# Attention and two mixtures of experts on one core: turns of the last batch behind P·V, the second mixture's first weights split during attention, first labels made in the tail

## The chip, the core and the metric

The program runs on one core of a Trainium2 chip. The metric is the device time in microseconds (us) of one execution, the median of several runs.

## The reference

Attention over 4 batches, 8 heads, 576 positions of 64 features, with a window of 32 (heads 0 to 3) or of 32 positions at a distance of 4 (heads 4 to 7); then a mixture in which every token goes to one expert by a greedy choice with a capacity; then a second mixture in which every token goes through all experts with balanced weights.

```python
scores = where(mask, q @ k.T / 8, -1e9)           # 4 x 8 x 576 x 576
x = softmax(scores) @ v                           # to 2304 tokens x 512
logits = x @ w_gate                               # 8 experts, 288 tokens each
for idx in argsort(-logits.flatten()):            # highest logit first
    ... token takes the expert if both are free
x = relu(x @ w1[e]) @ w2[e]                       # first mixture, e: the token's
P = exp(x @ w_gate2); 8 rounds of row and column normalization
out = sum over e of P[:, e] * (relu(x @ w1b[e]) @ w2b[e])   # second mixture
```

## The kernel before

All instructions are written out in order by hand (`manual_schedule`): each engine works through its own queue in program order, and waits come from the data that an instruction needs or the buffer that it writes. DMAs of SyncE (SP), ScalarE and GpSimd stand in the queue of the engine that issues them.

*Attention* works on 25 units. Unit u holds 96 queries of one block for the plain heads (kind 0, block u − 1) and 96 for the dilated heads (kind 1, block u), so that units 18 to 24 hold the last batch. The loop over n is a software pipeline: in step n come `scores(n)` (masks and q·k on TensorE), `row_max(n)` (the maximum and its product with −0.125, `nm`, on VectorE), `p_trans(n - 1)` and `p_evac(n - 1)` (transposes of the exponentials and their copy to `pt`), `exps(n)` (eight exponentials on ScalarE), `pv(n - 2)` (P·V, 16 matmuls, and the normalized rows `xt` on VectorE), and `x_out(n - 3)`, which splits `xt` into two f16 halves `xo`, the high one copied on ScalarE, the low one subtracted on GpSimd, and stores them to `xd` in DRAM. `xo` has two buffers. PSUM is divided among scores (`ps_s`, two), transposes (`ps_p`, one) and P·V (`ps_v`, one).

The q and k of all four batches are loaded ahead of the loop, `v` of two batches, the rest of `v` in steps 8, 9, 14, 15. Tokens' rows come back transposed from `xd` by a DMA transpose (`x_load`) for the first three batches, and `logits` of 128 tokens (12 matmuls) follow P·V in the steps after. For the last batch `x_turn` transposes `xo` on TensorE and copies it to `xl` on ScalarE. It does so for two units at a time at the end (`TURN`: in steps 24, 25 and 27; unit 22 in step 26). The last five chunks of logits are copied to `L` together.

*Routing.* `Router.phase(ph)` finds the tokens of one expert: labels (lines 455 to 460: the best logit `m` of each token, its expert as a code, the mask `A` of tokens), then six passes of a search for a threshold: G (line 476) compares `m` with 64 or 32 thresholds in two halves on VectorE, 18 matmuls count (line 480), `ok` compares the counts, a matmul hands `ok` to all partitions (line 485), `pen` and `cur` choose (lines 488 to 490). After the passes come the expert's index `widx` and the tokens' index `idx`.

*The mixtures* (`Moe.stage1`). During phase 0 TensorE has warming matmuls (`warm`, zeros) between the yields, and `weights` splits the first six of eight pieces of the second mixture's first expert: a DMA of 512 KB into `raw` (four buffers), the high half on ScalarE (line 679), the low one on VectorE (line 680). Then come gathers of the first mixture's weights (line 700) and of `x` (line 709) on GpSimd, 16 warming matmuls, and the first mixture's layers (`moe1`, line 731 the matmuls), interleaved with the next routing phase and the splits of the weights, the last two pieces of the second mixture's among them.

Of the kernel before, what the change touches and what calls it, by code (L numbers as in the profile page):

```python
# [83 lines left out]
TURN = {NU - 1: (NU - 7, NU - 6), NU: (NU - 5, NU - 4), NU + 2: (NU - 2, NU - 1)}  # L84
# [22 lines left out]
def attention(tc, q, k, v, masks, wg, ident, xd, L, zero):  # L107

    nc = tc.nc
    with ExitStack() as ctx:  # L110
# [24 lines left out]
        negc = one.tile([QB, 2, 4], F32)  # L135
        nc.gpsimd.memset(negc, -SC)
# [40 lines left out]
        def row_max(u):  # L177
            p, gs = SS[u], part(u, 4)
            nm = wk.tile([QB, 2, 4], F32, name="nm")
            nc.vector.tensor_reduce(nm[:, :, gs], p[:, :, gs], axis=AX.X, op=OP.max)  # L180
            nc.vector.tensor_mul(nm[:, :, gs], nm[:, :, gs], negc[:, :, gs])
            PP[u] = nm

        def exps(u):
            p, nm, gs = SS.pop(u), PP[u], part(u, 4)
            e = wk.tile([QB, 2, 4, 128], F32, name="e")
            for s in range(2):
                for g in range(gs.start, gs.stop):
                    nc.scalar.activation(e[:, s, g, :], p[:, s, g, :], AF.Exp, bias=nm[:, s, g:g + 1], scale=SC)
            PP[u] = e  # L190
# [15 lines left out]
        def pv(u, extra):  # L206
# [9 lines left out]
            fin = [logits(p[:, 0, 480 + E * n:480 + E * (n + 1)], c) for n, c in enumerate(extra)]  # L216
            rc = wk.tile([QB, 2, 4, 1], F32, name="rc")
            xt = wk.tile([QB, 2, 4, D], F32, name="xt")
# [4 lines left out]
            for f in fin:  # L223
                f()

        def x_out(u):
            xt, ks = XT.pop(u), part(u, 2)
            if u in XO:
                xo = XO[u]
            else:  # L230
                xo = wk.tile([QB, 2, 2, 4, D], F16, name="xo")
# [10 lines left out]
        def x_turn(*units):  # L242

            for u in units:
                p = ps.tile([128, 2, 512], F32, name="ps_s").bitcast(F16)[:, :, :4 * QB].rearrange(
                    "p k (c q) -> p k c q", c=4)
                ks = part(u, 2) if u > (B - 1) * NJ else slice(1, 2)
                for kind in range(ks.start, ks.stop):
                    for c in range(4):
                        nc.tensor.transpose(p[:, kind, c, :], XO[u][:, kind, c // 2, 2 * (c % 2):2 * (c % 2) + 2, :],  # L250
                                            idh)
                for kind in range(ks.start, ks.stop):
                    for o, n, tok, st in tokens_of(QB * UNITS[u][kind][1], QB, kind):
                        nc.scalar.activation(xl[kind][:, :, tok:tok + st * (n - 1) + 1:st], p[:, kind, :, o:o + n],
                                             AF.Copy)

        XB, XO = {}, {}
# [8 lines left out]
        def left(c, a, x):  # L266

            t0 = 128 * c - S * (B - 1)
            if x == 0:
                return XB[c][:, a, :]  # L270
            return xl[a // 4][:, a % 4, max(t0, 0):t0 + 128]

        def logits(p, c):
            cut = S * (B - 1) - 128 * c
            for x, rows in ((0, slice(0, min(cut, 128))), (1, slice(max(cut, 0), 128))):
                n = 0
                for kt in range(4 if rows.start < rows.stop else 0):
                    hi = kt if kt < 2 else kt + 2
                    for a, w in ((hi, wgh), (hi, wgl), (hi + 2, wgh)):
                        nc.tensor.matmul(p[rows], left(c, a, x), w[:, kt, :], start=(n == 0), stop=(n == 11))  # L280
# [7 lines left out]
        for b in range(1, B if True else 2):  # L288
            for kind in (1, 0):
                for nm in "kq":  # L290
                    load_qk(nm, b, kind)
            if b == 1:
                for kind in (1, 0):
                    load_v(b, kind)
        nc.scalar.activation(wgh, wgf, AF.Copy, scale=SG)
        nc.vector.scalar_tensor_tensor(wgl, wgf, SG, wgh, op0=OP.mult, op1=OP.subtract)
        xl = [one.tile([128, 4, S], F16, name="xl%d" % kind) for kind in range(2)]
        for n in range(NJ + 1):
            XO[(B - 1) * NJ + n] = one.tile([QB, 2, 2, 4, D], F16, name="xo%d" % n)
        first = S * (B - 1) // 128  # L300
        for n in range(NU + 3):
# [5 lines left out]
            if n < NU:  # L307
                exps(n)
            if n in FILL:
                warm(FILL[n])  # L310
            if n == NU + 1:
                x_turn(NU - 3)
            if 2 <= n <= NU + 1:
                pv(n - 2, [loaded.pop(0)[1] for _ in range(1 if n < NU else 2) if loaded and loaded[0][0] <= n])
# [3 lines left out]
            if n >= 3:  # L318
                x_out(n - 3)
# [9 lines left out]
            x_turn(*TURN.get(n, ()))  # L329
        p = ps.tile([128, 2, 512], F32, name="ps_v", bufs=1)  # L330
        rest = [i for _, i in loaded] + list(range(first, NT))
# [61 lines left out]
class Router:  # L393
# [39 lines left out]
    def start(self, ctx):  # L433
        self.wk = ctx.enter_context(self.tc.tile_pool(name="r_wk", bufs=2))

    def psum(self):
        return self.ps.tile([128, 512], F32, name=self.tag[0], bufs=self.tag[1])

    def phase(self, ph):
# [10 lines left out]
        if not last:  # L450
            m = wk.tile([128, NC], F32, name="m")
            w = wk.tile(full, F16, name="w")
            wm = wk.tile([128, NC], F32, name="wm")
            A = wk.tile(full, F16, name="A")
            V.tensor_reduce(m, Lm, axis=AX.X, op=OP.max)
            V.tensor_tensor(w, Lm, bc(m), op=OP.is_equal)
            V.tensor_mul(w, w, be(code))
            V.tensor_reduce(wm, w, axis=AX.X, op=OP.max)
            V.tensor_add(wm, wm, self.mask)
            V.tensor_tensor(A, w, bc(wm), op=OP.is_equal)  # L460
            cur, o = None, 0
            for n, bits in enumerate(STEPS):
# [8 lines left out]
                G = wk.tile([128, NC * 64], F16, name="G")[:, :NC * T].rearrange("p (c t) -> p c t", c=NC)  # L471
                p = self.psum()
                for h in range(2):
                    s = slice(h * NC // 2, (h + 1) * NC // 2)
                    sh = [128, NC // 2, T]
                    V.tensor_tensor(G[:, s], m[:, s].unsqueeze(2).to_broadcast(sh),
                                    c.unsqueeze(1).to_broadcast(sh), op=OP.is_ge)
# [126 lines left out]
class Moe:  # L604
    def __init__(self, ctx, tc, router, xd, ident, w1a, w2a, wg2, w1b, w2b, out, ps, zero):
        nc = self.nc = tc.nc
        self.tc, self.r, self.xd, self.out, self.ps = tc, router, xd, out, ps
# [3 lines left out]
        self.big, self.raw, self.sm = pool("m_big", 1), pool("m_raw", 4), pool("m_s", 1)  # L611
# [3 lines left out]
        self.acc = self.big.tile([128, NT, DM], F32, name="acc")  # L615
# [6 lines left out]
        self.W, self.balanced, self.scattered = {}, False, []  # L622
        self.wb = [[self.big.tile([128, 4, 7, 256], F16, name="w%d%s" % (n, c)) for c in "hl"] for n in (1, 2)]
# [11 lines left out]

    def psum(self):
# [692 lines left out]
```

## Time and profile before

| | us |
|---|---|
| median of 3 runs | 1833.92 (1832.78 to 1834.39) |
| profiled execution | 1835.58 |
| its span | 1833.8 |
| TensorE busy in it | 1752.4 (96%) |
| VectorE | 1371.8 (75%) |
| ScalarE | 838.0 (46%) |
| GpSimd | 226.7 (12%) |

The span runs from the first instruction to the last of the profiled execution; 1.78 us of its own time lie around it. The mean granted clock of TensorE is 0.979 of full speed. In the rows PE is TensorE's matmuls (PEld its weight loads), DVE VectorE, ACT ScalarE, POOL GpSimd, SP SyncE, and L174 line 174 of the kernel. Busy shares are means over stages with different limits. Attention fills about the first 127 us, the first routing phase ends near 162, and all that follows is the two mixtures.

### The profile page before, as it was taken

How to read it: one execution, taken by the hardware profiler on the slowest of the kernel's cores; microseconds unless marked ns; L12 is line 12 of the kernel's file. 1: busy time of each engine (PE TensorE's matmuls, PEld its weight loads, DVE VectorE, ACT ScalarE, POOL GpSimd, SP SyncE). 2: the span in 40 equal slices, each digit the busy share in tenths (PEclk: the TensorE clock that was granted, in tenths of full speed). 3: DMA queues.
4: the chain of work that ended last, by engine and by line, in shares of the span. 5: the costliest groups of instructions: out<-in, count | busy, mean ns of one | idle time of the engine just before them, and what ended most of it. 6: DMA issues, size and time to landing. Idle time of an engine off the chain costs nothing.

```text
span 1833.8 us, 35303 instructions
## 1 busy us (share of the span) xinstructions
PE 1752.4 (96%) x14518; PEld 1296.9 (71%) x14518; DVE 1371.8 (75%) x2625; ACT 838.0 (46%) x1502; POOL 226.7 (12%) x284
## 2 busy tenths in 40 slices
PE   8986898899999899999999999999999999999998
PEld 6873666676677657777777777777777777777776
DVE  5977776676744868887887888788878878887565
ACT  4662333333344345564544555444555544554333
POOL 1224222332221000000000000000000000000111
PEclk9987999999999999999999999999999999999999
DMA  8654322443343323434244432344352353433020
GB/s 304 149 137 134 114 83 77 127 119 94 87 142 94 88 82 150 152 132 160 99 167 178 170 139 108 154 155 157 131 205 101 109 213 147 155 132 151 35 96 35
DMA packets 106161, 241.19 MB, mean 132 GB/s; under 512 B 46704, under 2 KB 70512, under 8 KB 99088
## 3 DMA queue, kind: packets, MB, share of 16 engines
q1 hardware_dynamic: 84736, 151.34, 23.8%
q0 software_dynamic: 20592, 87.53, 13.7%
q8 instruction: 113, 1.85, 0.4%
q14 instruction: 48, 0.39, 0.1%
q10 hardware_dynamic: 672, 0.08, 0.0%
HBM read 173.83 MB, written 61.73 MB: 128 GB/s over the span
## 4 chain that ended last, share of the span: by engine, by line
PE 70%; issue 11%; DVE 10%; ACT 4%; DMA 3%; POOL 2%; SPq 0%; POOLq 0%; ACTq 0%; DVEq 0%
PE mm L995 26%; PE mm L1033 23%; PE mm L731 8%; PE mm L812 5%; PE mm L768 2%; PE ps_v L215 1%; DVE hl L952 1%; DVE w1l L680 1%; PE r L480 1%; PE ps_p L197 1%; PE ps_s L174 1%; POOL out_dram L1047 1%; ACT w1h L679 1%; DMA wgf<-in_wg_dram 1%; DMA rawk<-in_k_dram 1%
## 5 line engine op out<-in xcount | busy, mean ns | idle before, releaser
L995 PE MATMUL mm<-xb,w1h 128*128 128x384 f16 x2352 | 574.6, 327 | 5.9 <-DVE mm L966 5.0
L1033 PE MATMUL mm<-w2h,hh 128*128 128x256 f16 x1764 | 481.0, 273 | 1.3 <-DVE t L1057 1.2
L1033 PE MATMUL mm<-w2h,hl 128*128 128x256 f16 x1764 | 481.0, 273 | 0.0
L1033 PE MATMUL mm<-w2l,hh 128*128 128x256 f16 x1764 | 481.0, 273 | 0.0
L995 PE MATMUL mm<-xb,w1l 128*128 128x384 f16 x1176 | 384.2, 327 | 0.0
L1033 PEld LDWEIGHTS <-hh 128*128 128x128 f16 x3528 | 345.2, 98 | 43.9 <-issue 1.8
L995 PEld LDWEIGHTS <-w1h 128*128 128x128 f16 x2352 | 230.3, 98 | 160.9 <-issue 12.8
L1033 PEld LDWEIGHTS <-hl 128*128 128x128 f16 x1764 | 172.6, 98 | 20.0
L952 DVE TENSOR_TENSOR hl<-r,hh 128x1536 f16<-128x1536 f32 x84 | 147.5, 1756 | 42.4 <-ACT hh L951 42.4
L995 PEld LDWEIGHTS <-w1l 128*128 128x128 f16 x1176 | 115.2, 98 | 76.5 <-issue 0.7
L947 ACT ACTIVATE r<-mm 128x384 f32<-128x384 f32 x252 | 118.8, 480 | 96.8 <-PE mm L995 96.8
L951 ACT ACTIVATE hh<-r 128x1536 f16<-128x1536 f32 x84 | 124.6, 1483 | 48.4 <-DVE r L976 46.5
L913 POOL DMA_DIRECT2D ws<-raw x48 | 25.9, 541 | 945.4 <-ACT raw L864 724.2
L958 ACT ACTIVATE mm<-mm 128x384 f32<-128x384 f32 x84 | 40.3, 480 | 177.2 <-PE mm L995 177.2
L952 DVE TENSOR_TENSOR hl<-S,hh 128x1152 f16<-128x1152 f32 x84 | 113.5, 1352 | 0.0
L731 PE MATMUL mm<-xt,w1h 128*128 128x288 f16 x512 | 97.0, 289 | 1.4 <-ACT xt L745 1.4
L1043 DVE SCALAR_TENSOR_TENSOR acc<-t,P,acc 128x512 f32<-128x512 f32 x126 | 94.7, 752 | 4.5
L734 ACT ACTIVATE w1h<-mm 128x288 f16<-128x288 f32 (+1 forms) x120 | 46.8, 397 | 109.1 <-PE mm L731 91.0
L951 ACT ACTIVATE hh<-S 128x1152 f16<-128x1152 f32 x84 | 96.3, 1147 | 0.0
L735 DVE SCALAR_TENSOR_TENSOR w1l<-mm,w1h 128x288 f16<-128x288 f32 (+1 forms) x120 | 50.6, 436 | 56.2 <-ACT w1h L734 52.6
L864 ACT ACTIVATE raw<-raw 128x1024 f16<-128x1024 f32 x48 | 50.6, 1055 | 87.3 <-DVE raw L849 45.3
L731 PE MATMUL mm<-x2l,w0h 128*128 128x256 f16 x288 | 81.0, 281 | 8.4 <-DVE x2l L773 8.4
(258 smaller groups left out, 2970.0 us busy)
## 6 DMA issues: line engine op xcount, KB each, us to landing
xb<-xw SPq DMA_DIRECT2D x30, 1344.0 KB
ws<-raw POOLq DMA_DIRECT2D x48, 448.0 KB
ws<-r POOLq DMA_DIRECT2D x48, 448.0 KB
raw<-in_w2b_dram SPq DMA_DIRECT2D x32, 512.0 KB
raw<-in_w1b_dram SPq DMA_DIRECT2D x56, 256.0 KB
w1h<-ws SPq DMA_DIRECT2D x6, 1792.0 KB
w1l<-ws SPq DMA_DIRECT2D x6, 1792.0 KB
w2h<-ws SPq DMA_DIRECT2D x6, 1792.0 KB
```

Source lines behind the costliest of these rows:

```text
L731: nc.tensor.matmul(p, a[:, k, 128 * f:128 * (f + 1)], rhs(k, b), start=(k == 0 and i == 0), stop=(k == KT - 1 and i == 2))
L734: nc.scalar.activation(h[0][:, f, :n], p, AF.Relu)
L735: nc.vector.scalar_tensor_tensor(h[1][:, f, :n], p, 0.0, h[0][:, f, :n], op0=OP.max, op1=OP.subtract)
L812: nc.tensor.matmul(p, a[:, f, c], b[:, f, :], start=(f == 0 and n == 0), stop=(f == FT - 1 and n == 2))
L864: self.nc.scalar.activation(hi[:, k], x, AF.Copy, scale=sw)
L947: nc.scalar.activation(o, p, AF.Relu, scale=SH)
L951: yield nc.scalar.activation(hq[0][:, i, k], x, AF.Copy)
L952: yield V.tensor_sub(hq[1][:, i, k], x, hq[0][:, i, k])
L958: nc.scalar.activation(Q[i], P[i], AF.Copy)
L995: nc.tensor.matmul(p, w[u][:, 2 * j + i // 2, k, 128 * (i % 2):128 * (i % 2 + 1)], x[:, v, r, j], start=(q in (1, 5) and j == 0 and n == 0 ...
L1033: nc.tensor.matmul(p, h[u][:, i, a, 128 * t:128 * (t + 1)], w[v][:, i, b, :], start=(q in (1, 7) and i == 0 and j == 0), stop=(q in (2, 3) ...
L1043: V.scalar_tensor_tensor(self.acc[:, r, :], x, self.P[:, r, e:e + 1], self.acc[:, r, :], op0=OP.mult, op1=OP.add)
```

## The change

Before the loop of attention only the q and k of two batches are loaded, into two buffers each; the other two batches' are loaded in steps 6, 7, 12 and 13. `xo` has four buffers, `xt` three. `nm`'s product moves to ScalarE. `exps` yields after each half of its exponentials, and `x_out` stands between the halves. `x_turn` now transposes `xt` (f32) of one unit into free columns of a P·V or other PSUM bank and makes both f16 halves from there: copies on ScalarE, subtractions on VectorE. The turns of units 18 to 22 stand in `pv` of the unit after each (steps 21 to 25); those of 23 and 24 follow the loop. Chunks 13 and 14 of the logits may join the loop.

`first_weights` splits all eight pieces of the second mixture's first expert in attention: loads from step 4 on, then per step one half (512 columns) on ScalarE and the half before on VectorE. `Router.early` makes the labels and the first G of half of the columns between the last two turns; phase 0 makes the other half. `Moe` is made ahead of attention, with its load of `idf` and the copy `id16` on GpSimd. In phase 0 the splits go, and so do the single warming matmuls; three stand where five stood. Six stand where 16 stood ahead of the first mixture.

```diff
 def load_qk(nm, b, kind):
-    x = raw[nm, b, kind] = one.tile([128, 2, S], F32, name="raw%s%d%d" % (nm, kind, b))
+    x = raw[nm, b, kind] = ld.tile([128, 2, S], F32, name="raw%s%d" % (nm, kind))
...
 def row_max(u):
-    nc.vector.tensor_mul(nm[:, :, gs], nm[:, :, gs], negc[:, :, gs])
+    nc.scalar.activation(nm[:, :, gs], nm[:, :, gs], AF.Copy, scale=-SC)
...
-def pv(u, extra):
+def pv(u, extra, turn=None):
...
     fin = [logits(p[:, 0, 480 + E * n:480 + E * (n + 1)], c) for n, c in enumerate(extra)]
+    halves = x_turn(turn, p) if turn is not None else None
...
     for f in fin:
         f()
+    if halves is not None:
+        halves()
...
 def x_out(u):
+    xo = wk.tile([QB, 2, 2, 4, D], F16, name="xo", bufs=4)
     nc.scalar.activation(xo[:, ks, 0], xt[:, ks], AF.Copy)
-    eng = nc.gpsimd if u + 2 < NU else nc.vector
-    eng.tensor_sub(xo[:, ks, 1], xt[:, ks], xo[:, ks, 0])
+    nc.gpsimd.tensor_sub(xo[:, ks, 1], xt[:, ks], xo[:, ks, 0])
...
+def x_turn(u, p):
+    p = p[:, :, 264:264 + 2 * QB].rearrange("p k (c q) -> p k c q", c=2)
+    ks = part(u, 2) if u > (B - 1) * NJ else slice(1, 2)
+    for kind in range(ks.start, ks.stop):
+        for c in range(2):
+            nc.tensor.transpose(p[:, kind, c, :], XT[u][:, kind, 2 * c:2 * c + 2, :], idf[:QB, :QB])
...
+    def halves():
+        for n, (o, i, x) in enumerate(parts):
+            if x == 0:
+                nc.scalar.activation(o, i, AF.Copy)
+            else:
+                nc.vector.tensor_sub(o, i, hi[n - len(hi)])
+    return halves
...
-for b in range(1, B if True else 2):
-    for kind in (1, 0):
-        for nm in "kq":
-            load_qk(nm, b, kind)
+for kind in (1, 0):
+    for nm in "kq":
+        load_qk(nm, 1, kind)
...
-for n in range(NU + 3):
+for n in range(NU + 2):
...
-    if n < NU:
-        exps(n)
+    ex = exps(n) if n < NU else iter(())
+    next(ex, None)
+    turn = n - 3 if NU - 4 <= n <= NU else None
+    more = [loaded.pop(0)[1] for _ in range(1 if n < NU else 3) if loaded and loaded[0][0] <= n] if n >= 2 else []
+    if turn is not None:
+        pv(n - 2, more, turn)
+    if 3 <= n <= NU:
+        x_out(n - 3)
+    for _ in ex:
+        pass
     if n in FILL:
         warm(FILL[n])
...
+    if n >= 2 and turn is None:
+        pv(n - 2, more)
+    if 4 <= n:
+        next(side, None)
...
+    b, c = divmod(n - NJ, NJ)
+    if 0 <= b < B - 2 and c < 2:
+        for nm in "kq":
+            load_qk(nm, b + 2, 1 - c)
...
-    x_turn(*TURN.get(n, ()))
+    if n == NU:
+        loaded += [(n, i) for i in (first, first + 1)]
+turns = [x_turn(NU - 2, ps.tile([128, 2, 512], F32, name="ps_s")),
+         x_turn(NU - 1, ps.tile([128, 2, 512], F32, name="ps_p", bufs=1))]
+turns[0]()
+early()
+turns[1]()
+x_out(NU - 2)
+x_out(NU - 1)
...
 class Router:
+    def early(self):
+        half = slice(0, NC // 2)
+        self.pre = self.label_tiles(), self.grid(1 << STEPS[0])
+        self.labels(*self.pre[0], half)
+        self.above(self.pre[1], self.pre[0][0], self.thr[:, :1 << STEPS[0]].bitcast(F32), half)
...
 class Moe:
+    def first_weights(self, ctx):
...
+        for n in range(2):
+            load(n)
+        yield
+        for n in range(2, 4):
+            load(n)
+        yield
+        for n, (lay, k, per, m) in enumerate(todo):
+            r = live.pop(0).rearrange("p k f -> p (k f)")
+            hi, lo = (t[:, k:k + per, :].rearrange("p k f -> p (k f)") for t in self.W[("b", 0), lay])
+            for c in (slice(0, 512), slice(512, 1024)):
+                nc.scalar.activation(hi[:, c], r[:, c], AF.Copy, scale=(SW1, SW2)[lay])
+                yield
+                nc.vector.scalar_tensor_tensor(lo[:, c], r[:, c], (SW1, SW2)[lay], hi[:, c], op0=OP.mult,
+                                               op1=OP.subtract)
+                if c.stop == 1024 and n + 4 < len(todo):
+                    load(n + 4)
+        yield
...
     def stage1(self, ctx):
-        w0 = self.weights(("b", 0), "a", self.fetch_static(0), slice(6))
-        next(w0)
         for i, need in enumerate(self.r.phase(0)):
-            self.warm(1 if need < 2000 else 5)
-            if i % 2 and i < 14:
-                next(w0, None)
+            if need > 2000:
+                self.warm(3)
...
-        first = itertools.chain(fetched(0), self.weights(("b", 0), "a", self.fetch_static(0), slice(6, None)))
+        first = fetched(0)
...
-        self.warm(16)
+        self.warm(6)
...
-        attention(tc, q, k, v, masks, wg, ident, xd, L, router.zero)
-        moe = Moe(ctx, tc, router, xd, ident, w1a, w2a, wg2, w1b, w2b, out, ps, router.zero)
+        moe = Moe(ctx, tc, router, xd, ident, w1a, w2a, wg2, w1b, w2b, out, router.zero)
         with ExitStack() as stage:
+            router.start(stage)
+            attention(tc, q, k, v, masks, wg, ident, xd, L, router.zero, moe.first_weights(stage), router.early)
+            moe.after_attention(ctx)
             moe.stage1(stage)
```

## Rows read from the trace of the kernel before

**Rows 1.** The page: TensorE's busy share in 40 equal slices, tenths.
```profile
PE   8986898899999899999999999999999999999998
```

**Rows 2.** Stretch, length; busy of PE, PEld, DVE, ACT, POOL; clock, DMA share, GB/s.
```profile
24.00:36.00 12.00, 12.00 (x146) 10.94 (x145) 11.02 (x21) 7.25 (x26) 1.82 (x2) 1.00 1.02 411
36.00:48.00 12.00, 9.59 (x75) 8.15 (x75) 5.73 (x11) 5.84 (x19) 3.46 (x3) 0.72 0.26 85
```

**Rows 3.** Timeline of attention's start: start, duration, engine, line, operation, count, idle before.
```profile
15.06 0.23 ACT L295 ACTIVATE wgh<-wgf 128x32 f16<-128x32 f32 x1 [12.08 <-DMA wgf<-in_wg_dram]
...
34.43 1.21 DVE L180 TENSOR_REDUCE nm<-ps_s 96x8 f32<-96x1024 f32 x1
...
39.47 0.63 ACT L232 ACTIVATE xo<-xt 96x512 f16<-96x512 f32 x1 [4.66 <-DMA xd<-xo]
...
47.66 1.22 DVE L180 TENSOR_REDUCE nm<-ps_s 96x8 f32<-96x1024 f32 x1 [1.33 <-PE ps_s L174]
...
51.29 1.22 DVE L180 TENSOR_REDUCE nm<-ps_s 96x8 f32<-96x1024 f32 x1 [0.25 <-PE ps_s L174]
```

**Rows 4.** Chain of waits: start, us, what.
```profile
29.18 10.20 DMA xd<-xo
...
47.61 0.81 PE ps_p L197 x8
48.43 1.33 PE ps_v L215 x16
...
116.39 0.58 PE ps_v L280 x24
...
189.93 1.95 PE mm L731 x15
```

**Rows 5.** Timeline of a steady step, and of unit 24's reduction.
```profile
99.38 1.21 DVE L180 TENSOR_REDUCE nm<-ps_s 96x8 f32<-96x1024 f32 x1
...
99.56 0.65 ACT L232 ACTIVATE xo<-xt 96x512 f16<-96x512 f32 x1
...
100.28 1.16 POOL L234 TENSOR_TENSOR xo<-xt,xo 96x512 f16<-96x512 f32 x1 [2.88 <-ACT xo L232]
...
100.63 0.83 DVE L181 TENSOR_TENSOR nm<-nm,negc 96x8 f32<-96x8 f32 x1
...
101.38 0.94 DVE L204 COPY pt<-ps_p 128x768 f32<-128x768 f32 x1
...
101.57 2.14 ACT L189 ACTIVATE e<-ps_s,nm 96x128 f32<-96x128 f32 x8 [1.37 <-DVE nm L181]
...
102.25 0.15 DVE L219 TENSOR_SCALAR rc<-ps_v 96x8 f32<-96x8 f32 x1
...
111.47 0.68 DVE L180 TENSOR_REDUCE nm<-ps_s 96x4 f32<-96x512 f32 x1
...
112.18 0.16 DVE L181 TENSOR_TENSOR nm<-nm,negc 96x4 f32<-96x4 f32 x1
```

**Rows 6.** Timeline at the end of attention.
```profile
127.90 0.30 DVE L455 TENSOR_REDUCE m<-L 128x18 f32<-128x144 f32 x1 [0.20 <-DVE L L335]
...
130.50 1.30 PE L480 MATMUL r<-G,A 128*8 128x64 f16 x18 [0.46 <-DVE G L476]
...
132.28 0.23 PE L485 MATMUL r<-ok,ones 8*128 8x64 f16 x1
...
132.54 0.22 DVE L488 TENSOR_SCALAR pen<-r 128x64 f32<-128x64 f32 x1 [0.35 <-PE r L485]
```

**Rows 7.** Timeline of the first routing phase and the mixture's start.
```profile
139.32 1.20 DVE L680 SCALAR_TENSOR_TENSOR w0l<-raw,w0h 128x1024 f16<-128x1024 f32 x1
...
139.44 0.17 PE L485 MATMUL r<-ok,ones 8*128 8x32 f16 x1
...
140.45 0.17 DVE L488 TENSOR_SCALAR pen<-r 128x32 f32<-128x32 f32 x1
...
176.45 1.06 ACT L679 ACTIVATE w2h<-raw 128x1024 f16<-128x1024 f32 x1 [2.40 <-DMA raw<-in_w2a_dram,widx]
```

More of the change, by code (lines that the diff above doesn't have):

```diff
@@ L104, in lay_v, with attention @@
     return out
-def attention(tc, q, k, v, masks, wg, ident, xd, L, zero):
+def attention(tc, q, k, v, masks, wg, ident, xd, L, zero, side, early):
     nc = tc.nc
@@ L328, in attention @@
                 x_load(first, first + 1)
-            x_turn(*TURN.get(n, ()))
+            if n == NU:
[7 more added lines that the diff above has]
+        x_out(NU - 1)
         p = ps.tile([128, 2, 512], F32, name="ps_v", bufs=1)
-        rest = [i for _, i in loaded] + list(range(first, NT))
+        rest = [i for _, i in loaded] + list(range(first + 2, NT))
         o = p[:, 0, :E * len(rest)].rearrange("p (n e) -> p n e", e=E)
@@ L450, in phase @@
         if not last:
[L451 to L460, printed above, removed]
+            halves = [slice(h * NC // 2, (h + 1) * NC // 2) for h in range(2)]
+            if ph:
+                m, w, wm, A = tiles = self.label_tiles()
+                self.labels(*tiles, slice(0, NC))
+            else:
+                m, w, wm, A = self.pre[0]
+                self.labels(*self.pre[0], halves[1])
             cur, o = None, 0
@@ L470, in phase @@
                 c = c.bitcast(F32)
-                G = wk.tile([128, NC * 64], F16, name="G")[:, :NC * T].rearrange("p (c t) -> p c t", c=NC)
+                first = n == 0 and ph == 0
+                G = self.pre[1] if first else self.grid(T)
                 p = self.psum()
[L473 to L477, printed above, removed]
+                for s in halves[first:]:
+                    self.above(G, m, c, s)
                 yield 2600 if n else 4000
@@ L634, in __init__, with load @@
         self.h8 = [t[:, FLAT:FLAT + FT * 256].rearrange("p (f n) -> p f n", f=FT) for t in flat[1]]
+    def first_weights(self, ctx):
+        nc = self.nc
+        self.wp = ctx.enter_context(self.tc.tile_pool(name="m_w", bufs=1, side="right"))
+        live, fetch = [], self.fetch_static(0)
+        todo = [(0, k, 1, F) for k in range(KT)] + [(1, k, 2, DM) for k in range(0, FT, 2)]
+        for lay in range(2):
+            self.W[("b", 0), lay] = [self.wp.tile([128, (KT, FT)[lay], (F, DM)[lay]], F16, name="w%d%s" % (lay, c))
+                                     for c in "hl"]
+        def load(n):
+            lay, k, per, m = todo[n]
+            r = self.raw.tile([128, per, m], F32, name="raw")
+            fetch(lay, k, per, r)
+            live.append(r)
+        for n in range(2):
[14 more added lines that the diff above has]
+                    load(n + 4)
+        yield
     def psum(self):
@@ L643, in warm, with weights @@
             self.nc.tensor.matmul(p, self.zero[:, :128], self.zero, start=True, stop=True)
-    def weights(self, key, letter, fetch, some=slice(None)):
+    def weights(self, key, fetch):
         nc = self.nc
@@ L654, in weights @@
                 todo.append((lay, k, per, m))
-        todo = todo[some]
-        live, tiles = [], {lay: t for (k, lay), t in self.W.items() if k == key}
+        live, tiles = [], {}
         def load(it):
@@ L1148, in stage1 @@
     def stage1(self, ctx):
-        pool = lambda n, b: ctx.enter_context(self.tc.tile_pool(name=n, bufs=b))
-        self.r.start(ctx)
+        pool = lambda n, b: ctx.enter_context(self.tc.tile_pool(name=n, bufs=b, side="right"))
         self.xp = pool("m_x", 1)
```

116 lines of the change are left out of this document (51 added, 65 removed).

## The prediction

> **What bounds the kernel now.** I read TensorE's share by slices first. Of 40 slices of 45.8 us the fourth (137 to 183 us) is the lowest with six tenths, and from the ninth on nearly all hold nine [rows 1]; the change leaves that later part alone. So the chain of waits and the timeline of the first 200 us came next. Three stages stand out there.
>
> *Start of attention.* Until 36 us the DMA engines are saturated, at 411 GB/s [rows 2]. The stores of `xo` queue behind the q and k loads of all four batches: one issued at 29.18 lands 10.20 us later [rows 4]. `xo` has two buffers, so ScalarE, at 39.47, has waited 4.66 us for that store [rows 3], and all behind it stands.
>
> *The steady loop.* Three steps take 99.38 to 111.47 between reductions on VectorE, 4.03 each [rows 5]. TensorE's own need is the step from 47.66 to 51.29, 3.63, where the reduction waits for it [rows 3]: transposes 0.81, P·V 1.33 [rows 4], so scores 1.49. The nine steps with logits add 12 matmuls, half of 0.58 [rows 4]: 3.92. So VectorE sets the step: its starts are 1.25, 0.75, 0.87 and 1.16 apart, and the 0.75 is the tiny `nm` multiply, which takes 0.83 and ends with GpSimd's subtraction where that runs, and 0.16 where it doesn't [rows 5].
>
> *First routing phase.* Each pass goes G, count on TensorE, `ok`, broadcast, `pen`. Where a weight split (1.20) sits ahead of `pen`, broadcast to `pen` is 139.44 to 140.45, 1.01 us [rows 7]; without one, 132.28 to 132.54, 0.26 [rows 6].
>
> **The change part by part.** R(n) is the start of unit n's reduction; T its transposes.
>
> *A, loads and buffers.* Eight q and k tiles of 590 KB leave the opening burst: 4.7 MB, at 411 GB/s 11.5 us [rows 2]. It then ends near 24.5, before the first store is issued [rows 4]. The later loads (at most 1.3 MB of weights, q, k or v in a step, and 0.2 of stores) stay just under a step's 3.8 us times 411 GB/s = 1.56 MB, and four `xo` buffers cover a slow store. On SyncE's queue each load stands behind stores that wait for GpSimd, a step at most. R(6) = 34.43 to R(8) = 47.66 is 13.23 us [rows 3]; two steps of 3.63 are 7.26. The term is −6.0 (−5 to −6.5; TensorE's clock, 0.72 of full speed on average in 36 to 48 [rows 2], is in it). `idf`'s load and the copy `id16` now go ahead of the masks on SyncE's and GpSimd's queues. The first reduction stands on VectorE behind `wgl`, which needs `wgh`, and that waits for `wgf` until 15.06 [rows 3]: masks that come a little later are hidden by it. I take 0 (+1 if they come later still).
>
> *B, the loop.* `nm`'s multiply on ScalarE costs 0.23 by a 32-wide copy [rows 3]. The `xo` copy (0.65) moves between the halves of the exponentials (2.14) [rows 5], so reduction to last exponential is 1.21 + 0.1 + 0.25 + 2.14 + 0.65 = 4.35, and T ends at R + 4.55. Sixteen steps (7 to 22) get a split of 512 columns: some 0.63 on ScalarE (between 0.23 for 32 and 1.06 for 1024 columns [rows 3, 7]), done before the next `nm` is due; some 0.65 on VectorE (between 0.16 for 8 and 1.20 for 1024 [rows 5, 7]), last in the step. ScalarE's copy waits for its weight load, and behind it stand `nm` and the exponentials; the load is asked for two steps ahead at first and eight later, so 0. VectorE's sum is 1.17 + 0.87 + 1.16 + 0.62 = 3.82, near TensorE's 3.63 to 3.92, and `rc` waits for TensorE, so that the next R comes some 0.35 late. Two steps then cost 0.35 + 4.55 + 1.33 + 1.49 = 7.7 without logits, 8.0 with: 3.85 or 4.0 against 4.03, over 16 steps about −1. The turns of units 18 to 21 put up to four transposes (0.1 each [rows 4]), one to three copies of 0.33 (0.27 for 128 columns, 0.65 for 512 [rows 5]) on ScalarE and as many subtractions of some 0.35 on VectorE into steps 21 to 24, ahead of the second half of the exponentials: +1.5.
>
> The rest hangs on GpSimd. Its subtraction starts at R + 1.21 + 0.1 + 0.25 + 1.07 + 0.65 + 0.07 = R + 3.35; VectorE reaches the split at R + 3.2 to 3.4. If GpSimd is first and holds the split as it holds the multiply [rows 5], the split ends at R + 3.35 + 1.16 + 0.65 = R + 5.15 and the step loses 1.1; the next step reaches its split sooner and escapes. That leaves none to a third of the 16 steps; I take the middle, a sixth: +3. Bounds 0, and every step, +17.6. B = −1 + 1.5 + 3 = +3.5 (−2 to +18). The GPSIMD Engine Reference of the Trainium skill (section 8, Key points) says that GpSimd shares its SBUF interfaces with VectorE and contends with VectorE instructions that have two SBUF inputs. The split has two, `raw` and `hi`, so by that page any overlap costs time; the rows agree for the multiply (0.83 against 0.16), and none shows a split beside GpSimd.
>
> *C, the tail.* Before: R(24) = 111.47 [rows 5], labels at 127.90, 16.43 later, first count done at 131.80, 20.33 later [rows 6]. After, from R(24): T(23), P·V(22) and turn 21 end at 2.6; two copies, `xo` and two exponentials at 4.5; T(24), P·V(23), 24 logits and turn 22 at 7.1; `xt`(23) at 8.1 and turn 22's subtractions at 9.2; then chunk 13's logits, `xt`(24) at 10.4, turn 23 at 11.4. Now `early` is on VectorE: six ops on half the columns, 0.25 each (0.30 for the whole [rows 6]), and half of G, 2.2 in all; GpSimd's last subtractions (1.16 and less) fall into it and may hold up its two-input ops by 1 to 1.5. Behind it come turn 24's subtraction, the last logits and the copy: 15.9. The second half's labels, G and count add 1.5 + 0.7 + 0.7: 18.8. C = −1.5 (−4 to +2: most of it is estimated from sums).
>
> *D, first phase.* Five passes and the last broadcast lose their split: six times 0.75, −4.5 [rows 6, 7]. In the second pass the warming matmuls also stand ahead of the count; fewer of them give another 0.7. D = −5.2 (−4 to −6). The splits' work is in B, their loads in A.
>
> *E, start of the first mixture.* Six warming matmuls for sixteen free TensorE some 3 us sooner, but what is late is `w2h`, which waits for gathered weights until 176.45 [rows 7]; it hangs on the routing result and moves with it, so those 3 us turn into waiting. Two weight splits leave the first phase's layers (−1); a longer stretch at 1.2 GHz may come (+1). E = 0 (−2 to +3).
>
> Sum: −6.0 + 3.5 − 1.5 − 5.2 + 0 = −9.2. Later stages hang on these by dependences, so the end moves as much. The profiled execution took 1835.58: 1826.4. The median of the runs, 1833.92, is 1.66 lower: **1824.7**.
>
> **The rivals.** 1. *The split collides with GpSimd in every step* (slower). 17.6 takes the place of the 3: 1839. For it: the multiply met the subtraction in each steady step and lost [rows 5]. Against: a step that loses gives VectorE a head start in the next. It decides from some 0.8 us a step on. The page on GpSimd just cited stands on this side if overlaps are the rule.
> 2. *TensorE's clock eats it* (no change). With fewer warming matmuls the mixture's first matmuls might run at 1.2 GHz: 15 take 1.95 [rows 4], so the first 96 take 12.5 and would take 12.5 more, of which waiting for weights hides half: +6, 1831. For it: after ScalarE's stall, in which TensorE idled, the clock fell [rows 2]. Against: TensorE waits there in any case.
> 3. *No collision and a short tail* (faster still): B = 0, C = −4, D = −6: −16, 1818.
> 4. *A longer tail*: the turns and `early` delay the last logits, C = +2: 1828.
>
> **How the numbers follow.** Forecast 0.52, rivals 0.11, 0.12, 0.18 and 0.07. This measurement tells about 0.2%, 3.7 us, from no change: the limits are 1830.3 and 1837.6. Faster: forecast, rivals 3 and 4, 0.77. Same: rival 2 and the milder part of rival 1, 0.13. Slower: 0.10. The range 1815 to 1834 leaves out rival 1 and what lies beyond rivals 2 and 3.
>
> **What would show it.** A: no wait of ScalarE for a store, R(8) near 42. B: steps of 3.7 to 4.0 and 512-column splits of 0.65; splits of 1.2 or more beside GpSimd are rival 1. C: the first count done about 19 us after R(24). D: broadcast to `pen` 0.26 in every pass. E: the wait for gathered weights as long as before after the index, and the granted clock behind it. The prediction is wrong if ScalarE waits for a weight load, which stops exponentials, or if the first reduction comes later.

## The result and the profile after

The changed kernel takes 1845.99 us in the median of 4 runs (1843.92 to 1846.93), the kernel before beside it 1833.35: ratio 1.0071, 95% interval 1.0059 to 1.0083. It is slower by 12.6 us, where 1824.7 was forecast and 1834 was the range's upper end. The profiled executions' spans are 1842.1 and 1833.8; they differ by 8.3 only, since the profiled execution after lies 2.07 under its median and the one before 2.23 over its own. Where those 8.3 us came from is read at fixed points of both traces (R(n) is the start of unit n's reduction, `pen` the first of its kind in routing, `widx` the expert's index):

| stretch, up to | before | after | change in the stretch | forecast |
|---|---|---|---|---|
| R(8) | 47.66 | 43.01 | −4.65 | A −6.0 |
| R(20) | 95.36 | 92.01 | +1.30 | B without turns +2 |
| R(24) | 111.47 | 115.74 | +7.62 | B, turns +1.5 |
| first `pen` | 132.54 | 141.44 | +4.63 | C −1.5 |
| `widx` of phase 0 | 155.35 | 158.86 | −5.39 | D −5.2 |
| `widx` of phase 4 | 375.38 | 373.50 | −5.39 | E 0 |
| end of the span | 1833.8 | 1842.1 | +10.18 | none |

The stretch from R(20) to R(24) holds three of the four turns that the forecast priced there: the first turn stands in step 21, behind R(21).

The start went as forecast in kind. The page's TensorE slices have their gap where they had it [rows 1], and a second one has come in: the fifteenth slice (645 to 691 us) holds seven tenths, its neighbours eight. These are the two stretches of [rows 2], with the same columns: the burst of loads is over before 24 us (90 GB/s instead of 411), and the clock stays up from 36 to 48.

```profile
PE   8976898999999878999999999999999999999998
```

```profile
24.00:36.00 12.00, 12.00 (x146) 10.76 (x142) 9.96 (x16) 8.39 (x30) 2.99 (x3) 1.00 0.32 90
36.00:48.00 12.00, 12.00 (x142) 10.67 (x141) 11.03 (x19) 10.21 (x34) 4.59 (x3) 1.00 0.94 325
```

The timeline, against [rows 3]: no `xo` copy waits for a store any more, and R(8) is 4.65 earlier, though R(6) was 0.98 later. That 0.98 is this execution's: in the ten traces with this opening (after, e1 to e3, e5, e6, e8 to e11) R(6) lies between 34.38 and 35.72 and R(8) between 41.77 and 43.11; with the opening of before (before, e4) R(8) is 47.66 and 48.85.

```profile
35.41 1.22 DVE L176 TENSOR_REDUCE nm<-ps_s 96x8 f32<-96x1024 f32 x1 [0.38 <-PE ps_s L170]
...
41.55 0.63 ACT L229 ACTIVATE xo<-xt 96x512 f16<-96x512 f32 x1
43.01 1.21 DVE L176 TENSOR_REDUCE nm<-ps_s 96x8 f32<-96x1024 f32 x1
```

In the loop every split (L705) overlaps GpSimd's subtraction. In eleven of the steps 7 to 22 it takes 0.68 to 0.71 us and GpSimd is the one held; in steps 13, 16, 18, 20 and 22 the split is held, up to 1.69, and ends some 0.55 after GpSimd. Up to step 19 a step whose split is held takes 4.8 to 5.0 from one reduction to the next, the others 3.7 to 4.2.

```profile
77.89 1.28 POOL L230 TENSOR_TENSOR xo<-xt,xo 96x512 f16<-96x512 f32 x1 [2.11 <-DMA rawq<-in_q_dram]
78.03 1.69 DVE L705 SCALAR_TENSOR_TENSOR w1l<-raw,w1h 128x512 f16<-128x512 f32 x1
...
82.73 0.68 DVE L705 SCALAR_TENSOR_TENSOR w1l<-raw,w1h 128x512 f16<-128x512 f32 x1
82.85 1.58 POOL L230 TENSOR_TENSOR xo<-xt,xo 96x512 f16<-96x512 f32 x1 [3.68 <-DVE xt L219]
```

Steps 20 to 23 take 5.19, 4.99, 8.71 and 4.84, against 4.03 [rows 5]. Step 20 has no turn yet; its 5.19 is a held split:

```profile
95.22 1.51 POOL L230 TENSOR_TENSOR xo<-xt,xo 96x512 f16<-96x512 f32 x1 [2.12 <-ACT xo L229]
...
95.59 1.68 DVE L705 SCALAR_TENSOR_TENSOR w1l<-raw,w1h 128x512 f16<-128x512 f32 x1
...
98.18 0.36 PE L244 MATMUL ps_v<-idf,xt 96*128 96x96 f32 x2
```

The last row is the first turn's transposes. What follows them in step 21: a copy of the turn (L253) starts 0.09 after VectorE's copy of the logits (L277) has left the bank (its row names L194, which ended last but writes a bank that the copy does not read); `xo` and the exponentials (L186) stand behind it on ScalarE; the transposes (L194) wait 1.35 for them; and the P·V that follows, in step 22, takes 2.72 instead of 1.50, for the granted clock has fallen to half (0.50 from 104 to 108 in the windows). Step 22 has a held split besides (1.51 us).

```profile
100.30 0.15 DVE L277 COPY L<-ps_v 128x8 f32<-128x8 f32 x1
100.54 0.59 ACT L253 ACTIVATE xl<-ps_v 128x192 f16<-128x192 f32 x1 [0.73 <-PE ps_p L194]
100.88 0.68 ACT L229 ACTIVATE xo<-xt 96x512 f16<-96x512 f32 x1
...
101.46 1.11 ACT L186 ACTIVATE e<-ps_s,nm 96x128 f32<-96x128 f32 x4
...
101.86 1.16 PE L194 MATMUL ps_p<-idf,e 96*128 96x96 f32 x4 [1.35 <-ACT e L186]
...
102.81 2.72 PE L212 MATMUL ps_v<-rawv,pt 128*96 128x65 f32 x16
```

In the tail the granted clock is at half from about 116.3 us on, and a whole P·V takes 2.71. `early` (L452 and on) meets GpSimd (`w` takes 1.20 instead of 0.23), and the subtraction of the last turn (L255) stands behind `early` on VectorE, though its copy on ScalarE had been made at 132.77. The last logits wait 2.92 us for it:

```profile
116.75 2.71 PE L212 MATMUL ps_v<-rawv,pt 128*96 128x65 f32 x16
...
132.77 0.33 ACT L253 ACTIVATE xl<-ps_p 128x192 f16<-128x192 f32 x1
132.83 0.85 DVE L255 TENSOR_TENSOR xl<-ps_s,xl 128x192 f16<-128x192 f32 x2 [0.57 <-ACT xl L253]
...
133.69 1.78 POOL L230 TENSOR_TENSOR xo<-xt,xo 96x512 f16<-96x512 f32 x2 [2.25 <-DVE m L452]
...
133.73 1.20 DVE L453 TENSOR_TENSOR w<-L,m 128x72 f16<-128x72 f32 x1
...
136.21 0.75 DVE L462 TENSOR_TENSOR G<-m,thr 128x576 f16<-128x576 f32 x1
...
136.88 0.35 DVE L255 TENSOR_TENSOR xl<-ps_p,xl 128x192 f16<-128x192 f32 x1
137.29 0.22 PE L275 MATMUL ps_v<-wgh,xl 128*128 128x8 f16 x2 [2.92 <-DVE xl L255]
```

The routing phase went as forecast; broadcast to `pen` takes 0.22 in a later pass (146.76 to 146.98), against the 1.01 of [rows 7]:

```profile
146.76 0.18 PE L521 MATMUL r<-ok,ones 8*128 8x32 f16 x1 [0.33 <-DVE ok L518]
146.98 0.19 DVE L524 TENSOR_SCALAR pen<-r 128x32 f32<-128x32 f32 x1 [0.27 <-PE r L521]
```

The largest loss stands 500 us later. Where the second mixture begins, its first activations `xb` are asked for at 657.81; in the kernel before, the same load was issued at 640.86. TensorE waits for them twice, 7.2 us in all (timeline, then the waits of the stretch: engine, line, what it waited for, us in total, times, longest). SyncE had held the load (L996) for 19.4 us, until TensorE had left the layer before; that layer's last matmul (L882) ends at 657.78. The row of the wait names L718, warming matmuls that begin at 657.61.

```profile
657.81 0.82 SPq L996 DMA_DIRECT2D xb<-xw  x2
663.96 0.48 PE L1065 MATMUL mm<-xb,w1h 128*128 128x384 f16 x1 [4.89 <-DMA xb<-xw]
666.80 0.48 PE L1065 MATMUL mm<-xb,w1h 128*128 128x384 f16 x1 [2.36 <-DMA xb<-xw]
```

```profile
SPq L996 <- PE mm L718: 19.4, 1, 19.4
...
PE mm L1065 <- DMA xb<-xw: 7.2, 2, 4.9
```

### The profile page after: what moved, and what is told of

Same layout as the page of the kernel before. It is cut to its first block, busy times and chain, and to the rows that moved or that the text cites. A ratio compares the mean times of both kernels' runs of the same rounds, so it can differ in the third digit from the quotient of the medians.

```text
span 1842.1 us, 35241 instructions
## 1 busy us (share of the span) xinstructions
PE 1753.0 (95%) x14461; PEld 1298.7 (70%) x14461; DVE 1368.3 (74%) x2627; ACT 840.4 (46%) x1535; POOL 236.4 (13%) x285
## 4 chain that ended last, share of the span: by engine, by line
PE 68%; issue 12%; DVE 12%; ACT 4%; DMA 2%; POOL 2%; POOLq 0%; SPq 0%; ACTq 0%; DVEq 0%
PE mm L1065 26%; PE mm L1103 23%; PE mm L801 7%; PE mm L882 5%; PE mm L838 2%; DVE hl L1022 1%; PE r L516 1%; POOL out_dram L1117 1%; PE ps_v L212 1%; DVE G L462 1%; DVE w1l L750 1%; PE ps_p L194 1%; ACT raw L934 1%; DMA raw<-in_w2a_dram,widx 1%; DVE G L588 1%
```

## The experiments

Each row has the kernel before measured beside it; the last two columns are of the profiled execution. By the intervals, two rows have to lie some 4 us apart to be told from equal.

| | built on | median | before beside it | ratio (95%) | R(20) to R(24) | first `pen` |
|---|---|---|---|---|---|---|
| e1 | after | 1836.93 | 1833.98 | 1.0022 (1.0004–1.0040) | 22.95 | 138.71 |
| e2 | e1 | 1833.80 | 1833.98 | 1.0000 (0.9987–1.0013) | 21.85 | 137.84 |
| e3 | e2 | 1830.42 | 1833.98 | 0.9986 (0.9967–1.0004) | 21.15 | 135.61 |
| e4 | before | 1844.59 | 1833.98 | 1.0054 (1.0038–1.0071) | 16.14 | 133.94 |
| e5 | e3 | 1817.89 | 1832.49 | 0.9909 (0.9894–0.9925) | 26.30 | 138.82 |
| e6 | e5 | 1815.42 | 1832.49 | 0.9904 (0.9889–0.9919) | 15.49 | 122.82 |
| e7 | before | 1824.95 | 1832.49 | 0.9957 (0.9943–0.9970) | 16.11 | 127.75 |
| e8 | e6 | 1815.75 | 1832.49 | 0.9910 (0.9894–0.9925) | 15.50 | 123.62 |
| e9 | e6 | 1826.23 | 1832.53 | 0.9966 (0.9953–0.9979) | 19.97 | 132.62 |
| e10 | e6 | 1821.30 | 1832.53 | 0.9940 (0.9926–0.9954) | 17.40 | 130.73 |
| e11 | e6 | 1815.73 | 1832.53 | 0.9914 (0.9900–0.9927) | 15.50 | 124.62 |
| e12 | e7 | 1821.33 | 1833.40 | 0.9928 (0.9914–0.9942) | 15.44 | 124.47 |

**e1 and e4: the second mixture's start.** The pools of the second mixture are allotted in another order, so that `xb` (`n_x`) gets other addresses; e1 does it to the changed kernel, e4 the other way round to the kernel before.

```diff
-self.tp, self.bp, self.hp = pool("n_t", 1), pool("n_x", 1), pool("n_h", 1)
+self.bp, self.tp, self.hp = pool("n_x", 1), pool("n_t", 1), pool("n_h", 1)   # e1
+self.tp, self.hp, self.bp = pool("n_t", 1), pool("n_h", 1), pool("n_x", 1)   # e4
```

> The changed kernel with one edit: when the second mixture begins, the pool of xb is laid out ahead of the pool of its temporaries, so that xb takes other addresses. Theory: in the changed kernel xb's first load waited for the last matmul that reads the second mixture's first weights, whose addresses it takes, and that cost some 10 us between the first mixture's end and the second's first matmuls. Then the first load is issued near 638 to 642 us instead of 657.8, TensorE does not wait for xb (7.2 us before), and the time falls by 9 to 11 us to about 1835 to 1837. Rival: the start of the second mixture is late for the clock or because less was warmed up ahead; then the addresses do not matter and the time stays at 1846.

> The kernel before with one edit: the pool of xb is laid out last when the second mixture begins, so that xb takes addresses of the first mixture's last weights. Theory: the addresses alone cost the second mixture's start 9 to 11 us; then the time is 1842 to 1845 and TensorE waits some 7 us for xb. Rival: in the kernel before the start is bound by other waits, and the time stays at 1833 to 1835.

e1 is 9.1 us faster than the changed kernel, e4 10.6 slower than the kernel before. The load stands at 639.51 in e1, and TensorE no longer waits for it; in e4 it is issued at 661.15, and the waits of that stretch have the same row as after:

```profile
PE mm L995 <- DMA xb<-xw: 7.2, 2, 4.4
```

Addresses alone cost about 10 us in either kernel. By the sizes and the order of the pools `xb` takes the same bytes of a partition before and after, 164352 to 185856; what lay there has changed. Before, these bytes are tokens' tiles (`m_x2`) alone; after, they also hold `m_x` and the first 480 bytes of `m_w`, the tiles of the split weights, which now stand from 185376 on. `m_x` is read for the last time at 646.55, `m_w` by the layer that ends at 657.78, and the load is issued 0.03 after that. The 480 bytes belong to `w0h`, which was last read at 633.01: the load seems to have waited for the pool and not for the tile. In e4 `xb` lies under `m_w` for the most part, in e1 not at all (135168 to 156672). The overlap with `m_w` was not tried by itself.

**e2 and e3: the order on ScalarE and VectorE.** e2 lets the second half of the exponentials go ahead of the turn's P·V; e3 also emits the split ahead of P·V instead of behind it.

```diff
     if turn is not None:
+        for _ in ex:              # e2
+            pass
+        next(side, None)          # e3; without a turn likewise ahead of pv
         pv(n - 2, more, turn)
...
-    if 4 <= n:
-        next(side, None)
```

> As e1_xb_first, and in the steps with a turn all exponentials come before the turn on ScalarE's queue. Theory: the turn's copies wait for P.V, the turn and VectorE's normalization, and the second half of the exponentials stood behind them; TensorE then idled and fell to 1.2 GHz. Then R(20) to R(24) falls from 23.7 to 17 to 18.5 us, the clock there stays at 2.4 GHz, R(24) to the end of the first count falls from 25.1 to 19 to 21.5, and the time is 9 to 12 us under e1's. Rival: those steps are long because the splits collide with GpSimd and the turns add work to every engine; then the order on ScalarE gives less than 2 us.

> As e2_exps_before_turn, and the step's weight split is emitted ahead of P.V, so that VectorE does it after the copy of the transposes, before GpSimd's subtraction begins, instead of last in the step. Theory: every split in steps 7 to 22 takes 0.65 to 0.7 us, none 1.5 or 1.7, steps of 4.8 to 5.2 vanish, R(8) to R(20) falls from 49.0 to about 46 us, and the time is about 3 us under e2's. Rival: the normalization comes later for it, P.V's bank is free later and the step is as long as before on the average; then the time is within 1 us of e2's.

e2 brought 3.1 us, not 9 to 12: the four steps still take 21.85. With the exponentials out of the way another wait ended last, P·V for its bank. e3 brought another 3.4; all its splits take 0.68, but step 19 became 6.13 long, since its logits waited 1.19 for a chunk of `xT` from DRAM and the granted clock was at half behind that, up to 91.6. Its runs scatter from 1825 to 1839. Neither 3.1 nor 3.4 is clear of the intervals by itself; that the order of the split counts is shown by e10 below.

**e5, e6 and e9: the turns and the late chunk.** e5 puts the turns of before into e3 (`XO`, `TURN`, f16 transposes in a bank of the scores). e6 has e5's logits of the first two batches a step later. e9 is e6 with the turns of the change again.

```diff
-def pv(u, extra, turn=None):                     # e5; e9 takes this back
+def pv(u, extra):
...
-        loaded += [(n + 3, i) for i in range(c0, c1)]
+        loaded += [(n + 3 + (b < 2), i) for i in range(c0, c1)]      # e6, e9
...
+    x_turn(*TURN.get(n, ()))                     # e5
```

> e3 with the turns of the kernel before: 16-bit transposes of xo in a bank of the scores, one copy each on ScalarE, no turn inside P·V; everything else of e3 is kept. Theory (the turn makes P·V's single bank a chain TensorE -> VectorE -> ScalarE -> VectorE of about 5 us in each step): steps 20 to 24 fall from 21.2 us together to about 15.4 (3.85 each), the first count ends near 131, and the time is 5 to 9 us under e3's 1830.4, near 1823. Rival (steps 20 to 24 are slow for the clock and the labels' half in the tail, whatever the turns are): within 2 us of e3.

> e5 with the logits of the first two batches due one step later. Theory (in e3's step 19 TensorE waited about 2 us for a chunk of x that came back late from DRAM, which the steps without collisions brought closer): step 19 falls from about 6.1 to about 4, and the time is 2 us under e5's. Rival (the clock or a load makes that step long): as e5, within 1 us.

> e6 with the changed kernel's turns again (f32 transposes of xt inside P·V's bank in steps 21 to 25, halves from there by copies on ScalarE and subtractions on VectorE, the last two after the loop); nothing else differs from e6. Theory (the turn holds P·V's single bank for a chain through VectorE, ScalarE and VectorE, and TensorE falls to half clock while it waits): step 19 stays near 4, but steps 20 to 24 take 5 us each or more, some 20 to 23 us together against e6's 15.5, the first count ends 8 to 12 us after e6's 121.3, and the time is 8 to 14 us over e6's 1815.4. Rival (the late chunk of x at step 19 was what lowered the clock and made those steps long): steps 20 to 24 within 1 us of e6's and the time within 3 us of it.

e5's runs lie at 1813 to 1818 but for the profiled one, 1833.26. In that one TensorE waited for `xT` at step 19 and then ran at half clock for over 20 us, though it was busy without a gap (windows; the clock is the third number from the end):

```profile
89.86 0.19 PE L278 MATMUL ps_v<-wgh,xT 128*128 128x8 f16 x1 [2.86 <-DMA xT<-xd]
```

```profile
96.00:100.00 4.00, 4.00 (x40) 3.62 (x39) 1.41 (x5) 1.94 (x6) 1.15 (x1) 0.50 0.15 40
100.00:104.00 4.00, 4.00 (x28) 3.72 (x27) 2.78 (x3) 2.29 (x9) 0.36 (x1) 0.50 0.04 13
104.00:108.00 4.00, 4.00 (x38) 3.35 (x38) 1.54 (x5) 1.10 (x4) 0.80 (x1) 0.50 0.17 49
```

So the expectation of 15.4 us for those steps failed in that execution for a reason that has nothing to do with the turns. In e6 the wait is gone, the steps take 4.00, 3.95, 3.95 and 3.59, and all its runs lie within 2.6 us; the median is 2.5 us under e5's. The 2.5 is inside the intervals. In both profiles with the wait for `xT`, e3's and e5's, the clock falls at it (in e3 it is back at 1.00 from 92 on); in those without it (e6, e8 to e11) it stays at 1.00 from 84 to 108. That the wait is the cause, and that it is all of the scatter, is likely by this and not shown.

e9 then has the turns alone: step 19 stays at 3.70, the clock at 1.00 until 108 us, and still the steps take 4.00, 5.07, 5.45, 5.45. The first of these has no turn and is e6's; the three turns add 4.48 together, and R(24) to `pen` takes 24.59 for 19.95, 4.64 more. The first `pen` is 9.8 later than in e6 (0.68 of it was there at R(8)) and the time 10.8 longer. The chain in its timeline, from one P·V to the next:

```profile
97.47 1.54 PE L212 MATMUL ps_v<-rawv,pt 128*96 128x65 f32 x16 [0.52 <-DVE xl L255]
...
99.16 0.53 PE L244 MATMUL ps_v<-idf,xt 96*128 96x96 f32 x4
...
99.72 0.16 DVE L217 TENSOR_SCALAR rc<-ps_v 96x8 f32<-96x8 f32 x1
...
100.22 0.69 DVE L219 TENSOR_TENSOR xt<-ps_v,rc 96x512 f32<-96x512 f32 x1
100.83 0.15 DVE L277 COPY L<-ps_v 128x8 f32<-128x8 f32 x1
101.08 0.82 ACT L253 ACTIVATE xl<-ps_v 128x192 f16<-128x192 f32 x3 [0.34 <-DVE L L277]
...
101.93 0.85 DVE L255 TENSOR_TENSOR xl<-ps_v,xl 128x192 f16<-128x192 f32 x3 [0.95 <-ACT xl L253]
...
102.93 1.54 PE L212 MATMUL ps_v<-rawv,pt 128*96 128x65 f32 x16 [0.95 <-DVE xl L255]
```

P·V, logits and transposes, VectorE's three reads, ScalarE's copies, VectorE's subtractions: 5.46 us one behind the other in one bank, and the next P·V 0.15 after the last. The columns of the turn and of P·V are not the same, yet each waits for the other. The Trainium skill has the rule in "PSUM — Partial Sum Buffer" (section PSUM bank collisions raise a hardware error): no two engines may be at once on one bank in the same quadrant of its partitions, ScalarE and VectorE reading included, so that PSUM is guarded "by bank × quadrant", not by address. These rows agree: ScalarE's copies begin 0.10 after VectorE's last read ends. No run here shows two engines meeting in one bank.

**e7 and e12: two parts of the change alone.** e7 is the kernel before with the loads of q and k in steps 6, 7, 12, 13 and four `xo`. e12 has the product `nm` on ScalarE besides.

```diff
-x = raw[nm, b, kind] = one.tile([128, 2, S], F32, name="raw%s%d%d" % (nm, kind, b))
+x = raw[nm, b, kind] = ld.tile([128, 2, S], F32, name="raw%s%d" % (nm, kind))
...
-nc.vector.tensor_mul(nm[:, :, gs], nm[:, :, gs], negc[:, :, gs])
+nc.scalar.activation(nm[:, :, gs], nm[:, :, gs], AF.Copy, scale=-SC)     # e12
```

> The kernel before with one part of the change alone: q and k of the last two batches loaded in steps 6, 7, 12 and 13 into two buffers, and four buffers for xo. Theory (the early steps' delay in the kernel before is the traffic of the loads ahead of the loop and the second buffer of xo): the reduction of step 8 is 5 to 6 us earlier than in the kernel before (47.66), the end moves as much, ratio 0.997. Rival (what was gained early came from other parts of the change, or is lost again before the end of attention): step 8 within 1.5 us of before, ratio 1.000.

> e7 (the kernel before with the loads alone) with one more part: the product of the row maxima on ScalarE, 0.21 us there, instead of on VectorE, where it took 0.82 us beside GpSimd in every step of e7. Theory (this product, held up by GpSimd, sets the step of 4.03 us; without it a step is TensorE's own 3.7 us, 3.95 with a chunk of logits, as in e6): steps 8 to 20 take 45 to 46 us together against e7's 48.4, the first count ends 4 to 5 us earlier, and the time is 3 to 5 us under e7's 1825. Rival (VectorE's other work then falls beside GpSimd and is held up in its place): steps stay at 4.0 and the time within 1 us of e7.

e7: R(8) is at 42.28, 5.38 earlier, and the median 7.5 under before's. e12: steps 8 to 20 take 45.16 instead of 48.42, as the theory had it; the first `pen` is 3.28 earlier, for 4 to 5 (its R(6) came 1.51 late), and the median 3.6 lower, or 5.3 by the two ratios. In e7 the product takes 0.82 in each step and ends with GpSimd's subtraction; in e12 it takes 0.21 on ScalarE, and nothing on VectorE beside GpSimd is slowed: the copy `pt` keeps its 0.94.

```profile
75.48 1.16 POOL L234 TENSOR_TENSOR xo<-xt,xo 96x512 f16<-96x512 f32 x1 [2.88 <-ACT xo L232]
...
75.83 0.82 DVE L181 TENSOR_TENSOR nm<-nm,negc 96x8 f32<-96x8 f32 x1
```

```profile
77.22 1.15 POOL L232 TENSOR_TENSOR xo<-xt,xo 96x512 f16<-96x512 f32 x1 [2.80 <-DMA xd<-xo]
78.08 0.94 DVE L202 COPY pt<-ps_p 128x768 f32<-128x768 f32 x1
78.19 0.21 ACT L179 ACTIVATE nm<-nm 96x8 f32<-96x8 f32 x1 [1.04 <-DVE nm L178]
```

**e8, e10 and e11: three more parts, taken from e6.**

```diff
-self.warm(6)
+self.warm(16)                     # e8, ahead of the first mixture
...
     pv(n - 2, ...)
+    if 4 <= n:                    # e10: behind P·V, no longer ahead of it
+        next(side, None)
...
     nc.vector.tensor_copy(L[:, NT - len(rest):], o)
+    early()                       # e11: no longer ahead of the last logits
```

> e6 with 16 warming matmuls again instead of 6 ahead of the first mixture. Theory (the fewer warming matmuls gave the mixture its earlier start or shorter stretch, the 5.7 us between the first index and phase 3 in the changed kernel): 2 to 4 us over e6. Rival (those 5.7 us came from the splits of the second mixture's weights that no longer stand in the first mixture's first phases): within 1 us of e6.

> e6 with the split of the second mixture's weights emitted behind P·V, where the changed kernel has it, so that its subtraction on VectorE can fall together with GpSimd's subtraction in the same step. Theory (a collision costs the step about 1 us, in about a third of the steps): steps of 4.8 to 5.2 us come back in about five of the steps 8 to 20, those twelve steps take 3 to 4 us more than e6's 45.4, and the time is 2 to 4 us over e6. Rival (without the turns P·V is not late, and the split falls clear of GpSimd): within 1 us of e6.

> e6 with the labels and the first G of half of the columns made behind the last copy of the logits, so that no part of the first routing phase stands ahead of it. Theory (the half takes about 2.1 us of VectorE, 115.97 to 118.1 in e6, under TensorE's last logits): the first count ends about 2 us later, and the time is 1 to 3 us over e6. Rival (VectorE's half held up the copy of the last logits by 0.9 us, so that little was won): within 1 us of e6.

e8: the first mixture's first matmul comes 17.96 after `widx` instead of 15.30, but the layer of the second mixture that follows its two layers begins at 194.00 against 194.16; the time is the same. The fewer warming matmuls gave nothing that these runs can tell. e10: steps 14, 16, 18, 20 and 22 take 4.85 to 5.27 again, R(24) is 5.7 later, the time 5.9 longer: the order of the split is worth that much, more than the 2 to 4 expected. e11: the first `pen` is 1.80 later, and the time only 0.3 longer, inside the uncertainty, which takes in 1.8 as well. The `widx` of phase 3 is at 296.31 in e11 and at 296.60 in e6: in these two executions what labels made early win was gone by then. Whether that is so in all is not shown.

## Why the prediction was wrong

*A, loads.* Right: −4.65 at R(8), −5.38 alone (e7), for −6.0, and the scatter of R(8) over the traces is as large as what is missing. The cover that the text named for a later first step was gone, since `wgf` now landed at 5.97 instead of 15.06, the burst being shorter; yet the +1 that stood as a bound is not shown, for R(6), 0.98 late here, is 34.55 in e1, which has the same opening.

*B, the loop.* Two terms were mis-sized. `nm`'s move, inside the −1, is worth 3.6 us (e12; 3.26 of it in steps 8 to 20): rows 5 showed the multiply held by GpSimd in each step, and the sum put a like split in its place and found it almost even. The collisions, +3 for a sixth of the steps, cost 5.9 in e10; the split was held in every second one of the last ten steps, 5 of 16, which is the third that the text had as its most, and rival 1's "every step" is refuted: a step that loses does give the next one a start. In steps 8 to 20 the two nearly cancelled, +1.30.

Two steps of the prediction failed. The first is "The turns of units 18 to 21 put up to four transposes …: +1.5". It counted the engines' work and left out the bank: `ps_v` has one buffer, so a turn that lives in it puts its whole chain between two P·V. The stretch lost 7.62. Not all of that is turns: two of its splits were held (e10 loses 1.91 there against e6), and the exponentials stood behind the turn's copies, the first wait to show and not the last (1.10 there in e2). The bank alone is 4.48 for three turns, and turns and tail together are 10.8 in the time, by e9 against e6.

*C, the tail.* Forecast −1.5, came +4.63, by the same step: the sum lays the turns end to end with the engines' own times. It has turn 23 done 11.4 after R(24); it was 17.9, at 133.68. Each P·V took 2.71 at half clock, where the sum went by full clock, and each turn's chain stood in front of the next P·V. What the clock and the bank each have of these 6.5 us is not separated; in the kernel before the clock was at half too, from about 118.9. From there `early` and the last logits went as the sum had them, 4.3 for 4.5 up to the copy: GpSimd held `early` by 1.3, inside the 1 to 1.5 named, and the 2.92 that the last logits waited were in the sum. With the turns of before, R(24) to `pen` takes 19.95 (e6), without `early` 21.90 (e11), before 21.07. Rival 4 named this mechanism with +2.

*D, first phase.* Right: −5.39 for −5.2, from `pen` to `widx`.

*E, the mixture's start.* The sum 0 came out as −5.39, but most of it not by the edits: e7, whose mixtures are those of before, gains 4.14 in the same stretch (215.89 for 220.03), and in e8 the warming matmuls make no difference that the runs can tell, as was argued. The granted clock falls twice in phase 4 of before (between 320 and 330, and 340 and 350), once after. That goes with 1.7 us: phase 4 takes 60.03 and 60.13 in before and e4, with two falls, and 57.87 to 58.50 in the other twelve traces, with one or none. The rest, 3.7, stays open; single executions scatter by half of that (e4, which has the code of before up to there, takes 218.52, and e6 and e11, alike from the first `widx` on, differ by 2.0).

*The end.* The second step that failed, and the one that cost most, is "Later stages hang on these by dependences, so the end moves as much": +10.18 in the span, 9.1 by e1. It alone is not the whole miss: with it repaired e1 is at 1836.93, still above the range. No rival looked at where tiles come to lie. `Moe` made ahead of attention and all first weights split there change the allotment of SBUF, and a load into a reused address waits for that address's last reader.

From the changed kernel to e6 the medians fall by 9.1 (pools), 3.1 (exponentials), 3.4 (split), and then by 15.0 (turns of before and later logits), of which 10.8 are the turns (e9) and 4.2 the rest. Of these steps only the 9.1, the 15.0 and the 10.8 are clear of the intervals. e6 keeps the loads, `nm`, the early split and the routing phase of the change, and at 1815.42 beats both kernels, by 0.96% the one before (0.81 to 1.11).

## What to carry to other kernels

Work put into spare columns of a PSUM bank costs that bank's time, not its own: follow the bank from one owner to the next through every engine before counting instructions. After moving tiles between pools, list what shares their addresses in later stages, and look at when the first load of each later stage is issued. A VectorE instruction that is held by GpSimd in every step is worth moving even if it is tiny, and a larger one put in its place must begin before GpSimd does, as in e3 and e6.

## What was not expected of the hardware

Where a split with two SBUF inputs overlaps GpSimd's subtraction, in the changed kernel and in e10, the times look as if one of the two stood nearly still until the other is done: a held split ends 0.54 or 0.55 after GpSimd, whenever it began, and a held subtraction 1.01 to 1.03 after the split. All 14 splits that began 0.04 to 0.12 us ahead of GpSimd kept their 0.68 to 0.71. Of the 18 that began behind it 8 kept 0.68 too and 10 were held, up to 1.69; two pairs of the changed kernel, both 0.08 behind:

```profile
57.51 1.79 POOL L230 TENSOR_TENSOR xo<-xt,xo 96x512 f16<-96x512 f32 x1 [2.11 <-ACT xo L229]
57.59 0.68 DVE L705 SCALAR_TENSOR_TENSOR w0l<-raw,w0h 128x512 f16<-128x512 f32 x1
...
86.55 1.23 POOL L230 TENSOR_TENSOR xo<-xt,xo 96x512 f16<-96x512 f32 x1 [2.11 <-ACT xo L229]
86.63 1.69 DVE L705 SCALAR_TENSOR_TENSOR w1l<-raw,w1h 128x512 f16<-128x512 f32 x1
```

What decides there stays open. The GPSIMD Engine Reference of the Trainium skill (section 8, Key points), cited in the prediction, says that the two contend, and these rows agree. In e6, where the split begins 1.21 ahead, each keeps its own time, 0.68 and 1.16.

TensorE's clock, once it had fallen to 1.2 GHz at a wait of 2.86 us in e5, stayed there through more than 20 us of work without a gap, to about 116.9. The four other runs of that kernel, 1813 to 1818 us, are too short for such a loss.
